# Narrowing all of the first float64 matrix before the experts, and a third of batch 1 with more row buffers, fewer stores and a later start

## The chip, the cores and the metric

One core of a Trainium2 chip runs the kernel. The metric is the device time of one execution in microseconds (us). Names of the engines: PE is TensorE, DVE is VectorE, ACT is ScalarE, POOL is GpSimd, SP is SyncE, which here only issues DMAs.

## The reference, cut to what matters

```python
X = np.fft.rfft(x, axis=1)                      # x: (4, 3072, 256) float32
Yr = Xr @ w_r - Xi @ w_i + b_r                  # and Yi, both 256 x 256
Yr = np.sign(Yr) * np.maximum(np.abs(Yr) - lam, 0.0)
y = np.fft.irfft(Y, n=3072, axis=1)             # back to tokens, 12288 x 256
expert_idx = np.argmax(y @ w_gate, axis=1)      # 8 experts, the first 384 tokens of each are kept
h = np.maximum(np.einsum('ecd,edf->ecf', disp, w1), 0.0)
out = gate_w * np.einsum('ecf,efd->ecd', h, w2) # 256 -> 1024 -> 256, other rows zero
h = x @ w_in                                    # the second network: w_in, w_out are float64
return (h * (1.0 / (1.0 + np.exp(-h))) @ w_out).astype(np.float32)
```

The last three lines work on the rows that the experts kept. `moe2_w_in` (256 x 2048) and `moe2_w_out` (2048 x 256) come as float64 and are read as pairs of 32-bit words.

## The kernel before

The work runs in this order. **First spectra** (`near`): batch 0 of x is loaded and taken through the first stage of the transform, then `kphase(0)` forms 24 spectra in 12 steps (`forward`, `shrink`, `back`: products with tables on PE, splits on ACT and DVE), beside `s1(1)`, the first stage of batch 1. The inverse of batch 0 follows (`is2`), with gate logits for each token, and beside it the first steps of `kphase(1)`. `route` and `rank` then choose the tokens of the first three experts, while PE works off the rest of `kphase(1)`. **Experts** (`experts`): each expert is 8 steps of `first_ffn` (tile `hp`, then `y`), with float32 products made of three matmuls by `mm3` (L208 to L210) from a high and a low part of either factor. Experts 0, 1 and 2 come first, then `second_ffn` works on pairs of experts (products `h`, then `o`), between which experts 3 to 7 run. Beside experts 0 to 2 runs `third(1)`: the inverse transform of the first third of batch 1, in 4 passes of `rows` (two loads `br` of 384 KB of the spectra in DRAM, `b_d`; eight products; a copy to `ao`; stores to `attn`) and `gate`, and then its `route`.

**Narrowing.** `narrow` turns 512 float64 columns into float32: a load into a buffer `nt` (three of them; the tile `mt` takes turns in the same three), `na` on ACT (L874), and on DVE L875, L879, L880 and L881. `ffn_in` does this for the 8 parts of `moe2_w_in` and splits them into `wi` (ACT, then POOL); for each second part it also forms sums and differences `mt` on DVE (L911 to L914), which are stored to `mixed`. Parts 0 to 3 run beside the first spectra, 4 and 5 beside `is2`, and 6 and 7 in `experts` (generator `fi`, advanced at the steps in `FIRST`). `ffn_out` does the same for the 8 parts of `moe2_w_out` into `wo`, at the steps in `AHEAD` and in the first `second_ffn`.

**Weights of the experts.** `weights` loads quarters of w1 and w2 (256 KB each) into `st`, of which there are four buffers; ACT casts the high part into `w`, DVE or POOL makes the low part (L200). The load of an expert's weights waits on SP for `idi`, the expert's number.

**The order of the work.** A scheduler puts the instructions of each engine into one fixed order when the kernel is built; a pin `after(a, b)` moves `a` behind `b` in it. Each engine then works off its list in order and waits at the head of the list. SP's list holds nearly all DMAs, so a DMA that waits there holds up all behind it. In `experts` the counter `n` (one per step of `first_ffn`, nine steps an expert) says when a piece of the side work is recorded: `due` and the numbers that `beside` yields for the third, `AHEAD` for `ffn_out`.

`turn(rows, zeros, ...)` transposes the gathered tokens of an expert (tile `gtp`); for the first expert it also records six products of zeros into `pw` (L1079), which nothing reads. `pair` prepares two experts' outputs for `second_ffn` (tiles `m1` to `m4`, `b2`).

Of the kernel before, what the change touches and what calls it, by code (L numbers as in the profile page):

```python
# [9 lines left out]
F32 = mybir.dt.float32  # L10
FR = mybir.dt.float32r
# [5 lines left out]
B, S, D = 4, 3072, 256  # L17
N1, N2 = 48, 64
NK = 24
Q = 96  # L20
TW = 32
E, F, CAP = 8, 1024, 384
# [14 lines left out]
WARM = 11  # L37
FIRST = 1, 4
AHEAD = 7, 10, 13, 16, 20
PMS = "vav"  # L40
# [10 lines left out]
def _tables():  # L51
# [23 lines left out]
    c1 = np.einsum("akr,pz->apkrz", c1, eye2).reshape(Q, Q)  # L75
    third = np.einsum("kra,pz->krpza", c4[:, :, :QB // 2], np.eye(2)).reshape(Q, QB)

# [40 lines left out]
    ind = ind.transpose(1, 0, 2).reshape(2, 2 * P)  # L118
    u, q = np.arange(P) // QB, 2 * (np.arange(P) % 16) + np.arange(P) // 16 % 2
    at = TW * q + GT * u  # L120
# [35 lines left out]
class Kernel:  # L156
# [96 lines left out]
    def near(self):  # L253

        ads, self.bds, self.res = {}, {}, {}
        self.left = ExitStack()
        self.kp = self.left.enter_context(self.tc.tile_pool(name="kpa", bufs=2, reuse_waits="tile"))
        with self.stream("a", 3, "right"), self.sums("a", 2):
            self.warm()
            self.first()  # L260
            tables, spectra = self.load_tables(), self.kphase(0, ads)
            for g in (tables, spectra, tables, spectra, spectra):
                next(g)
            mix([tables, spectra, self.s1(1, ads), self.ffn_in(0, 4)], [4, 10, 24, 10], lead=[0, 0, 0, 0])
            rest = self.kphase(1, ads, True)
            next(rest)
            with self.tc.issue_after(self.fetched):
                self.route_consts()
            mix([self.is2(0, (0, 1, 2), self.res), self.ffn_in(4, 6, 5)], [10, 7])
            self.route(0, (0, 1, 2), self.res)  # L270
            self.rank()
            self.early = self.slots(self.cst, 0, EARLY, self.sel, "s")[0]
            for _ in rest:
                pass
# [290 lines left out]
    def third(self, b, res):  # L565
# [4 lines left out]
        bv = self.bds[b].rearrange("k (r u g) c -> (k r) u (g c)", r=4, u=4)  # L570
        od = self.attn[0][b * S:b * S + QB * TW].rearrange("(t p u g) d -> u p t (g d)", p=2, u=4, g=GT)
        res[b] = self.chosen(1)
        def rows(n):
            pt = ps.tile([P, CH], F32, tag="ps", name="ps2")
            for w in range(2):
                br = bp.tile([Q, 2, CH], F32, tag="xt", name="br", bufs=self.sb)
                nc.sync.dma_start(out=br, in_=bv[:, 2 * w:2 * w + 2, n * CH:(n + 1) * CH])
                for z in range(2):
                    u = 2 * w + z
                    ins = nc.tensor.matmul(pt[u * QB:(u + 1) * QB], c4, br[:, z], start=True, stop=True).ins  # L580
                    if b == 1 and not u:
                        self.after(ins, self.lasty)
            ao = bp.tile([P, 2, 2, P], F32, tag="ao", name="ao2")
            aof = ao.rearrange("p g h d -> p (g h d)")
            nc.scalar.copy(aof, pt)
            for u in range(4):
                for p in range(2):
                    at = u * QB + p * (QB // 2)
                    nc.sync.dma_start(out=od[u, p, :, n * CH:(n + 1) * CH], in_=aof[at:at + QB // 2])
            return ao  # L590
# [29 lines left out]
    def is2(self, b, qbs, res):  # L620
# [29 lines left out]
        def turn(ao):  # L650
            aT = bp.tile([P, 2, NB, P], F32, tag="aT", name="aT")
            for h in range(2):
                tp = ps.tile([P, 4, P], F32, tag="ps", name="tp")
                for x in range(4):
                    nc.tensor.transpose(tp[:, x], ao[:, x % 2, x // 2, h * P:(h + 1) * P], self.ident)
                for ch in range(2):
                    v.tensor_copy(aT[:, h].rearrange("c b (o x t) -> c o b x t", o=2, x=4)[:, ch],
                                  tp.rearrange("c x (o b t) -> c o b x t", o=2, t=T)[:, ch, qbs[0]:qbs[0] + NB])
            return aT
# [233 lines left out]
    def ffn_in(self, q0, q1, late=LATE):  # L893
# [5 lines left out]
        for q in range(q0, q1):  # L899
            h, z = q % 2, (q // 2) * W  # L900
            a = self.ffn_part([(self.i["moe2_w_in"][h * P:(h + 1) * P, z:z + W], slice(0, W))], None if self.again else self.evicted or self.shrunk, None if self.again else self.gated.get(q))
            a = a.rearrange("p (i f m) -> p i f m", f=2, m=P)
# [23 lines left out]
    def experts(self, again=False):  # L926
# [17 lines left out]
        def beside():  # L944

            with self.stream("b", 2, "left"):
                yield 4
                for n, _ in enumerate(self.third(1, self.res)):
                    yield 5 + 2 * n
                tiny = self.mc.tile([P, 1], F32, name="tiny")  # L950
# [5 lines left out]

        fw, fi = self.ffn_out(), self.ffn_in(6, 8, 0)
        if again:
# [12 lines left out]
        xg = {e: self.gather(e) for e in order[:2]}  # L971
        xs[0] = self.turn(xg.pop(0), None if again else 6)
        ws = {e: self.weights(e, n) for e, n in zip(order[:2], (3, 4))}
# [3 lines left out]
        for at, ph in enumerate(order):  # L977
# [11 lines left out]
            for m, _ in enumerate(part):  # L989
# [4 lines left out]
                while due is not None and due <= n:  # L994
                    due = next(side, None)
                if n in FIRST:
                    next(fi, None)
                if n in AHEAD or (ph == E and m < 3):
# [8 lines left out]
                if m == 6 and after < E:  # L1007
                    xs[after] = self.turn(xg.pop(after), 0, behind)
            if ph < E and ph > 1 and ph % 2:
# [53 lines left out]

    def turn(self, rows, zeros=0, behind=None):
        xg, gw = rows
# [5 lines left out]
        for h in range(2):  # L1071
            tp = self.ph.tile([P, CAP], F32, tag="hp", name="gtp")
            for j in range(SC):
                last = self.nc.tensor.transpose(tp[:, j * P:(j + 1) * P], xg[:, j, h * P:(h + 1) * P], self.ident)
            self.split("av", xT[:, 0, h], xT[:, 1, h], tp)
        if zeros:
            pw = self.pm.tile([P, 2 * D], F32, tag="y", name="pw")
            for n in range(zeros):
                self.after(self.nc.tensor.matmul(pw[:, :D], self.zt[:, 0, :P], self.zt[:, 0], start=True, stop=True).ins, last.ins)  # L1079
        return xT  # L1080
# [28 lines left out]
    def pair(self, behind=None):  # L1109
# [8 lines left out]

        def cut(nm, src):
            t = mg.tile([P, 2, CAP], FR, name=nm, bufs=1)  # L1120
            self.split("av", t[:, 0], t[:, 1], src)
            return t[:, 0], t[:, 1]
# [5 lines left out]
        v.tensor_tensor(t2, b[:, 1], t1, ALU.subtract)  # L1128
        m2 = cut("m2", t2)
        v.tensor_tensor(b[:, 0], b[:, 1], b[:, 0], ALU.subtract)  # L1130
        m3 = cut("m3", b[:, 0])
        m1 = cut("m1", t1)
        v.tensor_tensor(a[:, 1], a[:, 1], t2, ALU.subtract)
        m4 = cut("m4", a[:, 1])
        b2 = cut("b2", b[:, 1])
        if behind:
# [215 lines left out]
```

## Time and profile before

| | |
|---|---|
| median of three runs | 623.26 us (622.26 to 624.34) |
| the profiled execution | 623.3 us, span 621.5 us |
| busy, share of the span | PE 598.7 us (96%), DVE 420.3 (68%), ACT 338.8 (55%), POOL 197.1 (32%) |
| mean granted clock of TensorE | 0.993 |
| DMA | 86.09 MB, mean 139 GB/s |

The median of the runs and the profiled execution agree within 0.1 us. The span is what the trace covers; the 1.8 us around it are in the time of the execution. An engine's idle time costs something only where PE, the busiest engine, ends up waiting for it.

### The profile page before, as it was taken

The page shows a single profiled execution, that of the slowest core. Times are in us where ns is not written, and L with a number is a line of the kernel's source. Part 1 is how long each engine was busy: PE and PEld are TensorE (multiplying, and loading weights), DVE is VectorE, ACT ScalarE, POOL GpSimd, SP SyncE. Part 2 cuts the span into 40 slices and gives each one's busy share as a digit, 9 for nine tenths or more (in the row PEclk, how much of TensorE's full clock was granted, in tenths as well). Part 3 has the DMA queues.
Part 4 walks back from the last instruction along what each step waited for, and adds up shares of the span by engine and source line. Part 5 has one row for each costly group of instructions (what it writes and reads, how often), then busy time and mean ns, then how long its engine had stood idle before and what let it go on. Part 6 is the DMA issues. An engine that isn't in the chain of part 4 may idle for free.

```text
span 621.5 us, 11504 instructions
## 1 busy us (share of the span) xinstructions
PE 598.7 (96%) x4128; PEld 557.0 (90%) x4128; DVE 420.3 (68%) x838; ACT 338.8 (55%) x722; POOL 197.1 (32%) x195
## 2 busy tenths in 40 slices
PE   9999999999999987989999999999999999999994
PEld 9887899668986766969999999999999999999993
DVE  2454875359967677999877687576577577485562
ACT  2535654346524545556766657556567555475561
POOL 1000110002064331456744504446403443163433
PEclk9999999999999998999999999999999999999998
DMA  8738865986266877910553533403433130010001
GB/s 207 198 98 247 293 201 153 243 245 212 69 200 196 226 191 260 310 51 26 152 183 123 155 119 112 161 26 119 145 127 110 51 126 26 13 65 26 16 2 55
DMA packets 66012, 86.09 MB, mean 139 GB/s; under 512 B 6069, under 2 KB 55865, under 8 KB 65945
## 3 DMA queue, kind: packets, MB, share of 16 engines
q1 hardware_dynamic: 53976, 69.53, 37.4%
q10 hardware_dynamic: 9664, 9.44, 5.1%
q0 software_dynamic: 2304, 6.29, 3.2%
q8 instruction: 34, 0.56, 0.4%
q14 instruction: 34, 0.27, 0.2%
HBM read 54.31 MB, written 30.93 MB: 137 GB/s over the span
## 4 chain that ended last, share of the span: by engine, by line
PE 80%; DVE 8%; issue 5%; DMA 4%; SPq 1%; ACT 1%; POOL 0%; POOLq 0%; DVEq 0%; ACTq 0%
PE o L209 7%; PE o L210 7%; PE o L208 7%; PE h L208 6%; PE h L210 6%; PE h L209 6%; PE hp L210 3%; PE hp L209 3%; PE hp L208 3%; PE y L210 3%; PE yp L208 3%; PE y L208 3%; PE y L209 3%; PE yp L210 3%; PE yp L209 3%
## 5 line engine op out<-in xcount | busy, mean ns | idle before, releaser
L1250 DVE TENSOR_TENSOR u<-h,u 128x384 f32<-128x384 f32 x224 | 117.4, 551 | 55.5 <-PE h L210 50.2
L1173 ACT ACTIVATE u<-u 128x384 f32<-128x384 f32 x128 | 64.1, 521 | 70.0 <-DVE u L1250 69.4
L209 PE MATMUL o<-wo,gl 128*128 128x256 f32 x366 | 98.1, 281 | 0.6 <-DVE gl L200 0.6
L210 PE MATMUL o<-wo,gh 128*128 128x256 f32 x366 | 98.0, 280 | 0.0
L208 PE MATMUL o<-wo,gh 128*128 128x256 f32 x366 | 86.2, 280 | 0.1
L200 POOL TENSOR_TENSOR ring<-mt,ring 128x384 fp32r<-128x384 f32 x32 | 38.2, 1195 | 131.7 <-ACT ring L192 131.6
L200 POOL TENSOR_TENSOR gl<-u,gh 128x384 fp32r<-128x384 f32 x62 | 64.9, 1065 | 30.7 <-ACT gh L192 28.2
L209 PEld LDWEIGHTS o<-wo,gl 128*128 128x128 f32 x366 | 68.8, 188 | 1.5 <-DVE gl L200 0.9
L210 PEld LDWEIGHTS o<-wo,gh 128*128 128x128 f32 x366 | 68.8, 188 | 0.0
L192 ACT CAST gh<-u 128x384 fp32r<-128x384 f32 x126 | 63.4, 510 | 5.1 <-PE o L210 3.5
L208 PEld LDWEIGHTS o<-wo,gh 128*128 128x128 f32 x366 | 64.4, 188 | 0.4 <-ACT gh L192 0.4
L208 PE MATMUL yp<-wri,xk 128*128 128x256 f32 x188 | 56.0, 298 | 0.0
L1096 ACT ACTIVATE hh<-hp 128x384 fp32r<-128x384 f32 x64 | 31.1, 490 | 43.4 <-PE hp L210 22.7
L200 POOL TENSOR_TENSOR wi<-na,wi 128x256 fp32r<-128x256 f32 (+1 forms) x8 | 8.7, 1085 | 143.7 <-ACT wi L192 143.7
L209 PE MATMUL yp<-wri,xk 128*128 128x256 f32 x188 | 53.7, 286 | 0.0
L210 PE MATMUL yp<-wri,xk 128*128 128x256 f32 x188 | 53.6, 285 | 0.0
L1097 DVE SCALAR_TENSOR_TENSOR hl<-hp,hh 128x384 fp32r<-128x384 f32 x64 | 35.0, 551 | 26.6 <-ACT hh L1096 23.1
L192 ACT CAST w<-st 128x512 fp32r<-128x512 f32 x64 | 38.8, 620 | 23.8 <-DMA st<-in_moe_w 16.0
L200 DVE TENSOR_TENSOR w<-st,w 128x512 fp32r<-128x512 f32 x53 | 36.6, 701 | 17.4 <-ACT w L192 17.2
L208 PE MATMUL y<-hh,w 128*128 128x384 f32 x128 | 44.1, 344 | 3.1 <-ACT hh L1096 3.1
L210 PE MATMUL hp<-xT,w 128*128 128x384 f32 x128 | 43.3, 339 | 0.6 <-DVE xT L200 0.6
L209 PE MATMUL hp<-xT,w 128*128 128x384 f32 x128 | 43.4, 339 | 0.4 <-DVE w L200 0.4
(254 smaller groups left out, 1541.5 us busy)
## 6 DMA issues: line engine op xcount, KB each, us to landing
st<-in_moe_w SPq DMA_DIRECT2D x64, 256.0 KB, 3.1
out<-zt SPq DMA_DIRECT2D x48, 256.0 KB, 3.1
b_d<-bo ACTq DMA_DIRECT2D x12, 512.0 KB, 3.9
mt<-mixed SPq DMA_DIRECT2D x32, 192.0 KB, 2.4
xt<-in_x SPq DMA_DIRECT2D x15, 384.0 KB, 7.2
nt<-in_moe_w_in SPq DMA_DIRECT2D x8, 512.0 KB, 4.9
nt<-in_moe_w_out SPq DMA_DIRECT2D x16, 256.0 KB, 5.0
a_d<-ao SPq DMA_DIRECT2D x8, 384.0 KB, 4.2
```

The lines of the kernel that those rows point to most:

```text
L192: self.lastact = self.nc.scalar.copy(dst, src)
L200: return e.tensor_tensor(dst, src, raw(hi), ALU.subtract).ins
L208: first = nc.tensor.matmul(out, lh, rh, start=start, stop=False)
L209: nc.tensor.matmul(out, ll, rh, start=False, stop=False)
L210: return first.ins, nc.tensor.matmul(out, lh, rl, start=False, stop=stop).ins
L1096: self.rectified = nc.scalar.activation(hh, hp, AF.Relu).ins
L1097: self.evicted = nc.vector.scalar_tensor_tensor(hl, hp, 0.0, raw(hh), ALU.max, ALU.subtract).ins
L1173: act.activation(sg, sg, AF.Silu)
L1250: v.tensor_tensor(to, h, u, ALU.add)
```

## The change

It does the following:

- `ffn_in` takes parts 0 to 5 beside the first spectra, starting at once, and parts 6 and 7 beside `is2`; none is left for the experts, and `FIRST` goes. Its pins are changed to suit.
- `ffn_out` is recorded at steps 2, 5, 8, 12 and 16 of the experts, where it was at 7, 10, 13, 16 and 20.
- The third of batch 1 begins at step 7, where it began at 4, and its stages come at 8, 10, 12, 14 and 16. Four of its eight row loads go into buffers of their own: three into a tile `bi` that shares its place with the tile `ms` of `pair`, one into `by` in the place of `yT`. So six loads can be in flight, where it was two.
- The tokens of the third stand in another order on the partitions (table `third`, and `tri` and `tok` to match), so each pass stores four blocks of 32 rows (64 KB) where it stored eight of 16 rows. To fit this order `turn` inside `is2` lets PE write each transposed block to every second column of the tile `tp`, and the copy `aT` reads runs of 32 numbers, where they were 16.
- The six products of zeros `pw` go.
- `m1` to `m4` and `b2` become one tile `ms`.

```diff
-FIRST = 1, 4
-AHEAD = 7, 10, 13, 16, 20
+AHEAD = 2, 5, 8, 12, 16
...
-    third = np.einsum("kra,pz->krpza", c4[:, :, :QB // 2], np.eye(2)).reshape(Q, QB)
+    third = np.einsum("kra,pz->krpaz", c4[:, :, :QB // 2], np.eye(2)).reshape(Q, QB)
...
-            mix([tables, spectra, self.s1(1, ads), self.ffn_in(0, 4)], [4, 10, 24, 10], lead=[0, 0, 0, 0])
+            mix([tables, spectra, self.s1(1, ads), self.ffn_in(0, 6, 0)], [4, 10, 24, 7], lead=[0, 0, 0, 0])
...
-            mix([self.is2(0, (0, 1, 2), self.res), self.ffn_in(4, 6, 5)], [10, 7])
+            mix([self.is2(0, (0, 1, 2), self.res), self.ffn_in(6, 8, 5)], [10, 7])
...
+        idle = self.mg.tile([P, 3, 2, CH], F32, tag="ms", name="bi", bufs=1)
+        room = {n + 2: idle[:Q, n] for n in range(3)}
+        room[5] = self.mh.tile([P, 2, CH], F32, tag="yT", name="by", bufs=1)[:Q]
...
-                br = bp.tile([Q, 2, CH], F32, tag="xt", name="br", bufs=self.sb)
+                br = room.get(2 * n + w)
+                if br is None:
+                    br = bp.tile([Q, 2, CH], F32, tag="xt", name="br", bufs=self.sb)
...
-                for p in range(2):
-                    at = u * QB + p * (QB // 2)
-                    nc.sync.dma_start(out=od[u, p, :, n * CH:(n + 1) * CH], in_=aof[at:at + QB // 2])
+                nc.sync.dma_start(out=od[u, :, n * CH:(n + 1) * CH], in_=aof[u * QB:(u + 1) * QB])
...
-                tp = ps.tile([P, 4, P], F32, tag="ps", name="tp")
+                tp = ps.tile([P, 2, P, 2], F32, tag="ps", name="tp")
...
-                    nc.tensor.transpose(tp[:, x], ao[:, x % 2, x // 2, h * P:(h + 1) * P], self.ident)
+                    nc.tensor.transpose(tp[:, x // 2, :, x % 2], ao[:, x % 2, x // 2, h * P:(h + 1) * P], self.ident)
...
-                yield 4
+                yield 7
                 for n, _ in enumerate(self.third(1, self.res)):
-                    yield 5 + 2 * n
+                    yield 8 + 2 * n
...
-        fw, fi = self.ffn_out(), self.ffn_in(6, 8, 0)
+        fw = self.ffn_out()
...
-        xs[0] = self.turn(xg.pop(0), None if again else 6)
+        xs[0] = self.turn(xg.pop(0))
...
-                if n in FIRST:
-                    next(fi, None)
...
-        if zeros:
-            pw = self.pm.tile([P, 2 * D], F32, tag="y", name="pw")
-            for n in range(zeros):
-                self.after(self.nc.tensor.matmul(pw[:, :D], self.zt[:, 0, :P], self.zt[:, 0], start=True, stop=True).ins, last.ins)
```

How the lists of the engines move. Lines below L35 are numbered one less in the new kernel than the same line before, and a few shift by some more. **SP, just ahead of the first weights of the experts** (`ar` and `mixed` end the spectra, `idi` is the expert's number, `st` its weights). Before:

```order
L868 DMA nt_2178<-in_moe2_w_in 128x1024
L868 DMA nt_2282<-in_moe2_w_in 128x1024
L423 DMA ar_1911<-a_d1_428 128x4x256
L916 DMA mixed_74<-mt_1362 128x2x384
L1029 TENSOR_LOAD idi_1484
```

Now:

```order
L919 DMA mixed_74<-mt_1392 128x2x384
L422 DMA ar_1941<-a_d1_428 128x4x256
L871 DMA nt_2218<-in_moe2_w_out 128x512 x2
L871 DMA nt_2311<-in_moe2_w_out 128x512 x2
L871 DMA nt_2465<-in_moe2_w_out 128x512 x2
L1030 TENSOR_LOAD idi_1514
```

The last two parts of `w_in` have gone ahead of this place, and the first three parts of `w_out` stand here, where they stood among the loads of experts 0 and 1.

**SP, the row loads of the third** (`br`, `bi`, `by`), beside the weights of expert 0's last quarter and expert 1 (`st`). Before:

```order
L577 DMA br_2264<-b_d1_1019 96x2x512
L577 DMA br_2268<-b_d1_1019 96x2x512
L1038 ISA
L1038 DMA st_2318<-in_moe_w1 128x2x256
L577 DMA br_2329<-b_d1_1019 96x2x512
L1038 ISA
L1038 DMA st_2323<-in_moe_w2 128x2x256
L589 DMA attn0_71<-ao2_2272 16x512 x8
```

Now:

```order
L582 DMA br_2383<-b_d1_1049 96x2x512
L582 DMA br_2387<-b_d1_1049 96x2x512
L1039 ISA
L1039 DMA st_2301<-in_moe_w1 128x2x256
L582 DMA bi_2380<-b_d1_1049 96x2x512 x3
L582 DMA by_2381<-b_d1_1049 96x2x512
L1039 ISA
L1039 DMA st_2306<-in_moe_w2 128x2x256
L1039 ISA
L1039 DMA st_2340<-in_moe_w1 128x2x256
```

Four row loads in a row, where there was one, stand ahead of the second half of that quarter (`st_2306`, before `st_2323`), and the first stores come later and are four.

**PE, at the products of zeros**, between the first two quarters of expert 0 and its first `y`. Before:

```order
L209 MATMUL hp<-xT,w_2170 128x384
L210 MATMUL hp<-xT,w_2170 128x384
L1079 MATMUL pw<-zt 128x256 x6
L208 MATMUL y_2155<-hh,w_2136 128x384
L209 MATMUL y_2155<-hh,w_2136 128x384
```

Now:

```order
L207 MATMUL hp<-xT,w_2193 128x384
L208 MATMUL hp<-xT,w_2193 128x384
L209 MATMUL hp<-xT,w_2193 128x384
L207 MATMUL y_2178<-hh,w_2159 128x384
L208 MATMUL y_2178<-hh,w_2159 128x384
```

The `y` products follow the `hp` products directly.

## Rows read from the trace of the kernel before

**Rows 1.** The page: span, busy time of each engine, granted clock in 40 slices.

```profile
span 621.5 us, 11504 instructions
...
PE 598.7 (96%) x4128; PEld 557.0 (90%) x4128; DVE 420.3 (68%) x838; ACT 338.8 (55%) x722; POOL 197.1 (32%) x195
...
PEclk9999999999999998999999999999999999999998
```

**Rows 2.** Stretches: length, PE, PEld, DVE, ACT, POOL busy, clock, DMA share, GB/s.

```profile
25.00:125.00 100.00, 100.00 (x701) 83.47 (x701) 57.64 (x101) 48.20 (x102) 5.83 (x6) 1.00 0.68 196
...
225.00:250.00 25.00, 20.57 (x116) 16.75 (x115) 18.67 (x41) 13.26 (x28) 9.20 (x7) 0.93 0.80 235
...
300.00:600.00 300.00, 300.00 (x2041) 298.90 (x2040) 206.23 (x385) 182.80 (x393) 117.31 (x109) 1.00 0.30 95
```

**Rows 3.** Waits of PE from 175 to 300 us: total, times, longest.

```profile
PE y L208 <- ACT hh L1096: 3.1, 2, 2.4
PE ps L580 <- DMA br<-b_d: 1.1, 3, 0.5
PE h L210 <- DVE m L200: 1.1, 1, 1.1
PE y L210 <- DVE hl L1097: 1.1, 1, 1.1
PE gtp L1074 <- DVE xg L1067: 0.9, 1, 0.9
PE tp L596 <- ACT ao L585: 0.9, 1, 0.9
```

**Rows 4.** Waits of ACT and of DVE from 205 to 245 us.

```profile
ACT w L192 <- DMA st<-in_moe_w: 9.7, 4, 4.8
...
DVE nsg L879 <- DMA nt<-in_moe_w_out: 5.8, 3, 2.1
```

**Rows 5.** Timeline of SP: the four groups of stores (start, length).

```profile
200.03 4.41 SPq L589 DMA_DIRECT2D attn<-ao  x8
...
211.72 7.41 SPq L589 DMA_DIRECT2D attn<-ao  x8
...
223.61 8.98 SPq L589 DMA_DIRECT2D attn<-ao  x8
...
238.33 5.51 SPq L589 DMA_DIRECT2D attn<-ao  x8
```

**Rows 6.** The tile `attn`: issue of its stores, ns minimum/median/maximum.

```profile
L589 SPq DMA_DIRECT2D attn<-ao x32: 302/303/1238, 200.0 to 243.5; - x32
```

**Rows 7.** Timeline of PE at the products of zeros and behind.

```profile
190.09 2.75 PE L1079 MATMUL pw<-zt 128*128 128x256 f32 x12
192.50 0.52 PE L208 MATMUL y<-hh,w 128*128 128x384 f32 x1
```

**Rows 8.** Stretches, columns as above: expert 0's start, the clock's fall, the first pair.

```profile
180.00:190.00 10.00, 8.02 (x41) 6.43 (x40) 7.95 (x15) 4.41 (x9) 6.88 (x6) 1.00 0.66 204
...
235.00:240.00 5.00, 2.15 (x20) 1.45 (x18) 1.43 (x5) 1.83 (x5) 0.00 (x0) 1.00 0.93 294
240.00:244.00 4.00, 3.51 (x11) 3.52 (x12) 3.91 (x8) 2.89 (x7) 1.69 (x1) 0.57 0.81 285
...
260.00:280.00 20.00, 17.12 (x102) 14.98 (x101) 19.76 (x45) 10.29 (x24) 9.25 (x8) 1.00 0.25 79
```

**Rows 9.** DVE, 186 to 207 us by line: busy us, mean ns.

```profile
L880 DVE SCALAR_TENSOR_TENSOR na<-na,nsg 128x512 int32<-128x512 int32 x2 | 3.5, 1766 | 0.0
...
L913 DVE TENSOR_TENSOR mt<-mt,na 128x256 f32<-128x256 f32 x1 | 1.5, 1514 | 0.0
```

**Rows 10.** DMA, 192 to 255 us: the queue that SP issues into.

```profile
q1 hardware_dynamic: 11444, 14.55, 79.0%
```

**Rows 11.** The tile `tp` in `is2`: ns minimum/median/maximum.

```profile
L655 PE MATMUL tp<-ident,ao x64: 272/273/332, 117.1 to 144.9; 128*128 128x128 f32 x64
```

More of the change, by code (lines that the diff above doesn't have):

```diff
@@ L118, in _tables @@
     ind = ind.transpose(1, 0, 2).reshape(2, 2 * P)
-    u, q = np.arange(P) // QB, 2 * (np.arange(P) % 16) + np.arange(P) // 16 % 2
+    u, q = np.arange(P) // QB, np.arange(P) % QB
     at = TW * q + GT * u
@@ L570, in third @@
         bv = self.bds[b].rearrange("k (r u g) c -> (k r) u (g c)", r=4, u=4)
-        od = self.attn[0][b * S:b * S + QB * TW].rearrange("(t p u g) d -> u p t (g d)", p=2, u=4, g=GT)
+        od = self.attn[0][b * S:b * S + QB * TW].rearrange("(q u g) d -> u q (g d)", u=4, g=GT)
         res[b] = self.chosen(1)
+        idle = self.mg.tile([P, 3, 2, CH], F32, tag="ms", name="bi", bufs=1)
+        room = {n + 2: idle[:Q, n] for n in range(3)}
+        room[5] = self.mh.tile([P, 2, CH], F32, tag="yT", name="by", bufs=1)[:Q]
         def rows(n):
@@ L652, in turn @@
             for h in range(2):
-                tp = ps.tile([P, 4, P], F32, tag="ps", name="tp")
+                tp = ps.tile([P, 2, P, 2], F32, tag="ps", name="tp")
                 for x in range(4):
-                    nc.tensor.transpose(tp[:, x], ao[:, x % 2, x // 2, h * P:(h + 1) * P], self.ident)
+                    nc.tensor.transpose(tp[:, x // 2, :, x % 2], ao[:, x % 2, x // 2, h * P:(h + 1) * P], self.ident)
                 for ch in range(2):
-                    v.tensor_copy(aT[:, h].rearrange("c b (o x t) -> c o b x t", o=2, x=4)[:, ch],
-                                  tp.rearrange("c x (o b t) -> c o b x t", o=2, t=T)[:, ch, qbs[0]:qbs[0] + NB])
+                    v.tensor_copy(aT[:, h].rearrange("c b (o x w) -> c o b x w", o=2, x=2)[:, ch],
+                                  tp.rearrange("c x (o b t) p -> c o b x (t p)", o=2, t=T)[:, ch, qbs[0]:qbs[0] + NB])
             return aT
@@ L900, in ffn_in @@
             h, z = q % 2, (q // 2) * W
-            a = self.ffn_part([(self.i["moe2_w_in"][h * P:(h + 1) * P, z:z + W], slice(0, W))], None if self.again else self.evicted or self.shrunk, None if self.again else self.gated.get(q))
+            a = self.ffn_part([(self.i["moe2_w_in"][h * P:(h + 1) * P, z:z + W], slice(0, W))], None if self.again else self.shrunk, None if self.again else self.gated.get(q - 3))
             a = a.rearrange("p (i f m) -> p i f m", f=2, m=P)
@@ L1007, in experts @@
                 if m == 6 and after < E:
-                    xs[after] = self.turn(xg.pop(after), 0, behind)
+                    xs[after] = self.turn(xg.pop(after), behind)
             if ph < E and ph > 1 and ph % 2:
@@ L1062, in gather, with turn @@
         return xg, gw
-    def turn(self, rows, zeros=0, behind=None):
+    def turn(self, rows, behind=None):
         xg, gw = rows
@@ L1073, in turn @@
             for j in range(SC):
-                last = self.nc.tensor.transpose(tp[:, j * P:(j + 1) * P], xg[:, j, h * P:(h + 1) * P], self.ident)
+                self.nc.tensor.transpose(tp[:, j * P:(j + 1) * P], xg[:, j, h * P:(h + 1) * P], self.ident)
             self.split("av", xT[:, 0, h], xT[:, 1, h], tp)
-        if zeros:
-            pw = self.pm.tile([P, 2 * D], F32, tag="y", name="pw")
-            for n in range(zeros):
-                self.after(self.nc.tensor.matmul(pw[:, :D], self.zt[:, 0, :P], self.zt[:, 0], start=True, stop=True).ins, last.ins)
         return xT
@@ L1117, in pair, with cut @@
             self.split("av", out[k][0], out[k][1], a[:, k])
-        def cut(nm, src):
-            t = mg.tile([P, 2, CAP], FR, name=nm, bufs=1)
+        ms = mg.tile([P, 5, 2, CAP], FR, tag="ms", name="ms", bufs=1)
+        def cut(n, src):
+            t = ms[:, n]
             self.split("av", t[:, 0], t[:, 1], src)
@@ L1128, in pair @@
         v.tensor_tensor(t2, b[:, 1], t1, ALU.subtract)
-        m2 = cut("m2", t2)
+        m2 = cut(0, t2)
         v.tensor_tensor(b[:, 0], b[:, 1], b[:, 0], ALU.subtract)
-        m3 = cut("m3", b[:, 0])
-        m1 = cut("m1", t1)
+        m3 = cut(1, b[:, 0])
+        m1 = cut(2, t1)
         v.tensor_tensor(a[:, 1], a[:, 1], t2, ALU.subtract)
-        m4 = cut("m4", a[:, 1])
-        b2 = cut("b2", b[:, 1])
+        m4 = cut(3, a[:, 1])
+        b2 = cut(4, b[:, 1])
         if behind:
```

## The prediction, as it was made before the run

> **What bounds the kernel now.** I read the page first. PE is busy for 598.7 of 621.5 us, and no other engine for more than 68% [rows 1], so a change can only win where PE waits, computes for nothing, or runs at the lower clock. The stretches tell where. From 25 to 125 us (first spectra) PE is never idle, and neither is it from 300 to 600 us [rows 2]; work taken away from other engines there wins nothing. The idle time that this change can reach lies between, in the experts 0 to 2 and at the first pair: from 225 to 250 us alone PE is busy for 20.57 of 25 us [rows 2]. The list of PE's waits says for whom: `y` for `hh` 3.1 us in two waits, `y` for `hl` 1.1, the third's transposes `tp` for the copy `ao` 0.9, its row products for the loads `br` 1.1 [rows 3]. [...]
>
> The waits of ACT and DVE say why these come late. Between 205 and 245 us ACT stands for 9.7 us before casts of expert weights that have not landed, and DVE for 5.8 us before the narrowing of `w_out` parts that have not landed [rows 4]. Both lists are in order, so `hh` and `hl` stand behind these. And the loads are late because SP's list carries them between the third's stores: four groups of eight take 4.41, 7.41, 8.98 and 5.51 us from first to last [rows 5], though the issue of one is 0.303 us in the median [rows 6].
>
> **The change part by part.** The sum is made against the profiled execution of 623.3 us (span 621.5), which is the median of the runs, 623.26, to 0.1 us.
>
> *Products of zeros, removed.* Twelve instructions from 190.09 to 192.50, where the next product, `y`, starts [rows 7]: 2.4 us on PE. By the timeline of ACT and DVE, what that `y` needs (weights and `hh`) was there before they ended, so I take 2.4 us as won. The bounds are 0 (the time becomes a wait) and 2.4. They may have held up the clock: before them PE is idle for 2.0 of 10 us at a granted clock of 1.00 [rows 8]. [...] I go by the row, since the products only fill time that real work now takes.
>
> *Parts 6 and 7 of `w_in`, moved out of the experts.* In expert 0 their narrowing costs DVE 3.5 us in L880 and 1.5 us in L913 alone [rows 9], with the rest of its lines between `hl`s. The first spectra get two more parts. There DVE is busy for 57.64 and ACT for 48.20 of 100 us [rows 2], and the first two loads now go out when the transfers of x end; the cover is the slack of DVE and ACT, and if it failed, `xk` would be late for PE. I charge 0.2 us.
>
> *Stores halved, `w_out` loads pulled ahead of the experts.* The four groups of stores take 4.41 + 7.41 + 8.98 + 5.51 = 26.3 us of SP's list [rows 5]. Half as many take between 16 x 0.303 = 4.8 us less, by the issue alone [rows 6], and 13.2 us less, half the groups; I take the upper end, since the groups show what SP really spends. Three parts of `w_out` (1.5 MB) leave the stretch from 192 to 255 us, where SP's queue moves 14.55 MB [rows 10], or 231 GB/s: 6.5 us of transfers. Each of the waits for weights and for `w_out` that hold `hh`, `hl` and `ao` is at most 4.8 us long [rows 4], so loads earlier by this much end them: 3.1 + 1.1 + 0.9 = 5.1 us of PE's waits [rows 3]. With the wait of 2.4 us goes the fall of the clock. In its stretch PE is busy for 3.51 us at 0.57 [rows 8], which costs 3.51 x 0.43 = 1.5 us.
>
> *More row buffers, third later.* The rows can't be loaded before batch 1's spectra are in DRAM, and that doesn't change; but PE now has three steps more of expert 0 before it needs them. The 1.1 us of waits for `br` [rows 3] go. Against this, four row loads now stand in one piece ahead of the second half of a weight quarter, three more than before: 3 x 384 KB at 231 GB/s are 5.1 us by which those weights and the ones behind may be late. The PE list puts some 24 expert products and a transposition ahead of the first that needs them. Between 0 and 5.1 us I take half, 2.5.
>
> *Ahead of the first expert.* The wait of `gtp` for the gathered tokens, 0.9 us [rows 3], stays: the change's list asks for the first tokens a little earlier and has spectra products behind. I charge 0.5 us, within a bound of 1.9 either way, which is nearly all that PE is idle there [rows 8].
>
> *The first pair.* From 260 to 280 us PE is idle for 20 - 17.12 = 2.9 us while DVE is busy for 19.76 of 20 [rows 8]; the largest wait there is `h` for a split of `pair`, 1.1 us [rows 3]. DVE comes to it with less left over from narrowing, but PE comes earlier too. I take half, 1.4 us, between 0 and 2.9. That `m1` to `m4` share one tile costs nothing: the next pair is prepared after the last one's products.
>
> *Transposes to every second column.* 64 instructions of 273 ns [rows 11], as many as before, with as many columns. No row shows PE writing with a step. The bounds are 0 and a start-to-start time doubled from some 0.147 us, which is 9.4 us; I take 0, because each still writes one number per column and partition.
>
> Sum: 2.4 + 5.1 + 1.5 + 1.1 + 1.4 - 0.2 - 2.5 - 0.5 = 8.3 us, so 623.3 - 8.3 = **615.0 us**. Its own range is 609.5 to 619.
>
> **The rivals.** *The bandwidth, not the list, holds the weights (0.15).* If SP's saved time only lets loads queue at the DMA engines, half of the 5.1 us and the clock's fall remain: 615.0 + 2.5 + 1.5 = 619. For it: from 235 to 240 us the DMA share is 0.93 at 294 GB/s [rows 8]. Against it: three `w_out` parts have left that stretch. [...]
>
> *DVE is the bound and takes it back (0.09).* If the first pair can't start earlier because `route` and `pair` fill DVE whatever PE does, what the experts win comes back as a wait there; only the products of zeros and part of a wait are won, and the charges take these: 622 to 623. For it: 19.76 of 20 us [rows 8]. Against: DVE stood for 5.8 us before loads [rows 4], and what it did not do then, it did here.
>
> *The burst of rows starves expert 0 and 1 (0.08, the other side).* Place: SP's list behind the four row loads; price: the weights come L later, PE waits for them, and a wait like that of 2.4 us brings one fall of the clock, 1.5 us. The waits of before stay, so only 2.4 + 1.1 = 3.5 us are won: 623.3 - 3.5 + L + 1.5. It is slower than before from L = 2.0 us on, and by over 0.3% from 3.9. With 5.1 us of rows and as much again as the stores' share, some 6.6 us, it gives 628.
>
> *The stepped transposes cost what their upper bound says (0.03):* 615.0 + 9.4 = 624.4.
>
> **How the numbers follow.** The forecast has 0.65, the rivals 0.15, 0.09, 0.08 and 0.03. A measurement of this kernel can tell about 0.3% (1.9 us) from no change. Faster by more, below 621.4: the forecast and the first rival, 0.80. Within it: the second and the last, 0.12. Slower: 0.08. The range reaches from 609.5, nearly all of the waits won, to 621.5, which takes in the first rival and part of the second.
>
> **What would show it.** Right: PE's busy time falls by 2 to 5 us and its wait for `hh` below 1 us; the granted clock is 1.00 from 225 to 250 us; no wait of DVE for `w_out` above 1 us; groups of four stores below 4 us each; expert 0 begins within 2 us of where it began, and the first `o` comes about 8 us earlier. From there on the traces run in parallel. Wrong, if PE waits for `w` around 200 us, if the first spectra show idle time of PE, or if `tp` takes longer than 273 ns each.

## The result, and the profile after

The changed kernel takes **615.84 us** in the median of six runs (613.65 to 618.49), the kernel before 622.95 beside it (622.21 to 625.84): a ratio of **0.988**, with a 95% interval from 0.985 to 0.991. 615.0 was forecast, so the sum came out. Its terms did not all: two came out wrong, two were missing, and these nearly cancelled. One execution of the kernel before and one of c_both (below) ran over 1.5% above the fastest of their kernel and are left out of the figures below.

The profiled execution has a span of 614.2 us, 7.3 less than before. The page:

```profile
span 614.2 us, 11459 instructions
...
PE 593.2 (97%) x4116; PEld 553.2 (90%) x4116; DVE 420.4 (68%) x838; ACT 338.7 (55%) x722; POOL 196.8 (32%) x195
...
PEclk9999999999999999999999999999999999999998
```

PE's busy time fell by 5.5 us [rows 1], but its idle time only from 22.8 to 21.0. Stretches of the span (columns as in [rows 2]):

```profile
25.00:125.00 100.00, 100.00 (x702) 83.47 (x702) 63.27 (x112) 50.70 (x107) 8.35 (x9) 1.00 0.71 207
125.00:150.00 25.00, 22.78 (x211) 14.57 (x211) 17.74 (x48) 11.93 (x25) 2.73 (x3) 1.00 0.69 211
...
200.00:205.00 5.00, 3.96 (x26) 2.47 (x25) 3.91 (x9) 1.90 (x5) 0.61 (x1) 1.00 1.07 249
205.00:210.00 5.00, 4.21 (x23) 3.56 (x21) 1.58 (x3) 1.77 (x4) 0.69 (x1) 1.00 1.08 260
210.00:215.00 5.00, 3.31 (x15) 1.70 (x15) 3.36 (x6) 2.69 (x6) 1.93 (x2) 0.78 1.09 272
215.00:220.00 5.00, 5.00 (x39) 3.80 (x35) 4.09 (x6) 2.80 (x6) 2.36 (x2) 0.88 0.94 250
225.00:250.00 25.00, 24.76 (x161) 21.98 (x158) 21.72 (x53) 13.19 (x29) 9.78 (x9) 1.00 0.82 258
...
250.00:275.00 25.00, 22.83 (x140) 21.02 (x139) 24.72 (x59) 13.89 (x30) 10.08 (x10) 1.00 0.21 64
```

The first spectra still leave PE no idle time, although DVE is busier there (63.27 us for 57.64). The stretch from 225 to 250 us, the worst before, is nearly full and runs at a clock of 1.00. In exchange there are new holes: 2.22 us from 125 to 150 us, where it was 0.57 (the row of before stands below), and 3.5 us from 200 to 215 us, with the DMA engines at a share above 1.0. Behind them the granted clock falls, to 0.78 and 0.88 in two stretches. So the fall of [rows 8] has not gone; it comes 28 us earlier. The inverse of batch 0 before:

```profile
125.00:150.00 25.00, 24.43 (x238) 17.51 (x236) 17.55 (x51) 12.46 (x28) 2.47 (x3) 1.00 0.76 227
```

The waits of PE from 195 to 215 us and, below the gap, from 25 to 150 us (total, times, longest):

```profile
PE y L207 <- ACT w L191: 1.8, 1, 1.8
PE hp L207 <- ACT w L191: 0.7, 1, 0.7
PE hp L207 <- DVE hl L1094: 0.5, 1, 0.5
PE y L209 <- DVE hl L1094: 0.3, 1, 0.3
...
PE lg L671 <- DVE aT L660: 1.2, 2, 0.7
PE tp L658 <- DVE L L557: 1.0, 1, 1.0
```

The waits for `hh`, `ao` and `br` [rows 3] are gone, and those for `hl` are 0.8 us. Those for `w`, 2.5 us, are new, and so are 2.2 us beside the inverse of batch 0, where parts 6 and 7 of `w_in` now make DVE late with `L` and `aT`. Behind the waits for `w` stand casts whose weights have not landed: ACT waits for `st` for 10.0 us between 205 and 245 us, where it was 9.7 [rows 4], and for 13.0 from 200 us on.

SP's list, the four groups of stores of the third:

```profile
208.11 3.58 SPq L592 DMA_DIRECT2D attn<-ao  x4
...
220.90 2.35 SPq L592 DMA_DIRECT2D attn<-ao  x4
...
225.28 2.06 SPq L592 DMA_DIRECT2D attn<-ao  x4
...
234.16 2.17 SPq L592 DMA_DIRECT2D attn<-ao  x4
```

They take 10.2 us, not 26.3 [rows 5]: half as many stores, and less than half the time. Why less than half shows in the waits of SP before, from 199 to 244 us, and in its list around the third group of stores:

```profile
SPq L589 <- DMA nt<-in_moe_w_out: 5.7, 10, 1.1
SPq L589 <- DMA br<-b_d: 3.7, 4, 1.1
SPq L589 <- DMA st<-in_moe_w: 2.9, 5, 1.0
```

```profile
219.37 1.06 SPq L1038 DMA_DIRECT2D st<-in_moe_w  x2
220.47 0.94 SPq L868 DMA_DIRECT2D nt<-in_moe_w_out  x2
221.52 0.37 SPq L577 DMA_DIRECT2D br<-b_d  x1
222.13 0.39 SPq L1038 DMA_DIRECT2D st<-in_moe_w  x1
222.57 0.47 SPq L868 DMA_DIRECT2D nt<-in_moe_w_out  x1
223.14 0.37 SPq L577 DMA_DIRECT2D br<-b_d  x1
223.61 8.98 SPq L589 DMA_DIRECT2D attn<-ao  x8
```

Of the 26.3 us, 12.3 are not issue but waits of stores for earlier loads to land. The last six stores of the third group wait, by the profile, for `nt`, `nt`, `br`, `st`, `nt` and `br`: in each case the DMA that stands eight places ahead in the list. In the trace the 276 DMAs of SP's list have eight semaphores between them, and each of these six stores waits for the DMA that had its semaphore before. The eight stores of a group have all eight, one each, so here a store of 32 KB took up one of eight places just as a load of 384 KB did.

A gain that the prediction doesn't have shows in PE's own products of the third. Timeline of PE before, the first four groups of row products, and of the change, its first and last:

```profile
196.76 1.05 PE L580 MATMUL ps<-br,c 96*32 96x512 f32 x4 [0.43 <-DMA br<-b_d]
198.32 1.05 PE L580 MATMUL ps<-br,c 96*32 96x512 f32 x4 [0.52 <-DMA br<-b_d]
...
203.35 1.05 PE L580 MATMUL ps<-br,c 96*32 96x512 f32 x4
...
208.66 1.05 PE L580 MATMUL ps<-br,c 96*32 96x512 f32 x4 [0.19 <-DMA br<-b_d]
```

```profile
202.01 1.11 PE L585 MATMUL ps<-br,c 96*32 96x512 f32 x8
...
229.31 1.06 PE L585 MATMUL ps<-br,c 96*32 96x512 f32 x8
```

Before, the four instructions of one load (two products, each of two) take 1.05 us, and the four of the pass's other load 1.05 us more at another time: eight such groups, 8.4 us. With the change both loads of a pass are there, the list puts all eight together, and they take 1.06 to 1.11 us: they write four different strips of 32 partitions of `ps2`, and PE overlaps them (in the first pass the products into all four strips start within 0.07 us). The four passes take 1.11, 1.94 (in the stretch of the lower clock), 1.24 and 1.06, together 5.4 us. That is 3.1 us won (8.42 - 5.35).

### The profile page after: what moved, and what is told of

It is laid out like the page before. It is cut to its first block, busy times and chain, and to the rows that moved or that the text cites. A ratio compares the mean times of both kernels' runs of the same rounds, so it can differ in the third digit from the quotient of the medians.

```text
span 614.2 us, 11459 instructions
## 1 busy us (share of the span) xinstructions
PE 593.2 (97%) x4116; PEld 553.2 (90%) x4116; DVE 420.4 (68%) x838; ACT 338.7 (55%) x722; POOL 196.8 (32%) x195
## 2 busy tenths in 40 slices
DMA packets 65755, 86.09 MB, mean 140 GB/s; under 512 B 5812, under 2 KB 55608, under 8 KB 65688
## 5 line engine op out<-in xcount | busy, mean ns | idle before, releaser
L199 DVE TENSOR_TENSOR w<-st,w 128x512 fp32r<-128x512 f32 x53 | 38.4, 734 | 18.5 <-ACT w L191 14.0
L207 PE MATMUL y<-hh,w 128*128 128x384 f32 x128 | 43.5, 341 | 1.8 <-ACT w L191 1.8
L207 PE MATMUL hp<-xT,w 128*128 128x384 f32 x128 | 43.4, 340 | 1.4 <-ACT w L191 0.7
L208 PE MATMUL y<-hh,w 128*128 128x384 f32 x128 | 43.3, 338 | 0.0
```

The lines of the kernel that those rows point to most:

```text
L199: return e.tensor_tensor(dst, src, raw(hi), ALU.subtract).ins
L207: first = nc.tensor.matmul(out, lh, rh, start=start, stop=False)
L208: nc.tensor.matmul(out, ll, rh, start=False, stop=False)
```

## The experiments

All were timed against the kernel before in five rounds. The interval of a ratio is about 0.0025 either way, so two kernels differ for certain only from some 0.004, 2.5 us, on. Each run also lists its mean granted clock, which scatters from 0.98 to 0.997 between runs of one kernel (a_layout). Time x (1 - clock) is my estimate, from these two figures of a run, of what the lower clock can have cost, at most, and time x clock is the rest. Both are means over the runs of a kernel, and the standard error of the last column is about 0.5 us or less where none is given. The kernel before alone has 619.0, 618.4 and 617.7 us there in the rounds of the runs a_zeros to a_ahead, a_noroom to b_layout, and c, so that between these groups a difference of 1 us says nothing.

| kernel | ratio to before (95%) | mean clock | time x (1 - clock) | time x clock |
|---|---|---|---|---|
| before (40 runs) | 1 | 0.991 | 5.3 | 618.4 |
| the change | 0.988 (0.985 to 0.991) | 0.993 | 4.4 | 611.4 |
| a_zeros | 0.994 (0.992 to 0.996) | 0.991 | 5.9 | 614.3 |
| a_layout | 0.993 (0.991 to 0.996) | 0.992 | 5.3 | 614.4 (1.2) |
| a_first | 0.987 (0.985 to 0.990) | 0.993 | 4.6 | 611.4 (0.7) |
| a_ahead | 0.992 (0.989 to 0.994) | 0.990 | 6.0 | 612.6 |
| a_noroom | 0.993 (0.990 to 0.995) | 0.992 | 4.7 | 614.3 |
| a_start4 | 0.989 (0.987 to 0.992) | 0.994 | 3.7 | 613.4 |
| b_nozeros | 0.997 (0.995 to 0.999) | 0.990 | 6.2 | 616.0 |
| b_layout | 0.992 (0.990 to 0.995) | 0.995 | 3.4 | 615.2 |
| c_laynoz | 0.992 (0.990 to 0.995) | 0.992 | 5.1 | 613.4 |
| c_all8 | 0.990 (0.987 to 0.994) | 0.990 | 6.2 | 610.9 (0.9) |
| c_rows | 0.987 (0.984 to 0.990) | 0.991 | 5.4 | 610.2 |
| c_both | 0.987 (0.984 to 0.991) | 0.993 | 4.4 | 610.4 (1.5) |

**The products of zeros** (a_zeros: back into the changed kernel; b_nozeros: taken out of the kernel before).

```diff
-        xs[0] = self.turn(xg.pop(0))
+        xs[0] = self.turn(xg.pop(0), None if again else 6)
```

> The changed kernel with the six products of zeros put back into `turn`, nothing else. Theory (the term of the sum, 2.4 us of PE): the twelve instructions push back all behind them, so the time is 615.8 + 2.4 = 618.2 us, 0.992 of before. Rival (they only fill a wait for the first weights, so the span from the first `hp` to the first `y` stays as long as it is): 615.8 us, 0.988. A fall of the clock that they prevent would show as a time below 615.8.

> The kernel before without the six products of zeros, nothing else. Theory (PE time of their own): 2.4 us less than 623, 0.996 of before. Putting them back into the changed kernel cost 0.6%; if that was more than their own time, because what is behind them is then late in other ways, it is 0.994 here too. Rival (they fill a wait): 1.000.

Putting them back costs 0.6% of the time before, some 3.9 us, and taking them out of the kernel before wins 0.3%, 1.8 us, with an interval from 0.5 to 3.1. With the clock taken out, that is 2.9 and 2.4 us. So they cost their own time, and the rival that they fill a wait falls. In a_zeros PE then waits 5.2 us for `w` in one piece. Whether they hold up the clock stays open: without them the cost of the lower clock is 0.9 us higher in b_nozeros (6.2 for 5.3), but with them it is 1.5 us higher in a_zeros (5.9 for 4.4).

**Half the stores** (a_layout: the old order of tokens in the changed kernel; b_layout: the new one alone in the kernel before).

```diff
-                for p in range(2):
-                    at = u * QB + p * (QB // 2)
-                    nc.sync.dma_start(out=od[u, p, :, n * CH:(n + 1) * CH], in_=aof[at:at + QB // 2])
+                nc.sync.dma_start(out=od[u, :, n * CH:(n + 1) * CH], in_=aof[u * QB:(u + 1) * QB])
```

> The changed kernel with the old order of tokens: eight stores of 16 rows for each pass of the third, and transposes in `is2` that write whole columns. Theory (SP's list holds the weights): SP gets back up to 13 us of stores and the weights of experts 0 and 1 come later, so PE waits 3 to 5 us more: 619 to 621 us, 0.994 to 0.997 of before. Rival (the DMA engines hold them; their share is 1.0 and more from 195 to 215 us in the trace of the change): within 1 us of 615.8, 0.987 to 0.990. If writing every second column of PSUM costs PE anything, the transposes of `is2` are shorter here than 273 ns.

> The kernel before with the new order of tokens alone: half the stores of the third, transposes of `is2` to every second column. Theory (SP's list holds the weights): 3 us less, 0.995 of before, as undoing it in the changed kernel cost 0.5%, and the wait of 2.4 us for `hh` at 240 us gets shorter. Rival (the loads of `w_out` and the narrowing of `w_in` in the experts hold `hh` here, whatever SP spends on stores): within 1 us, 0.9985 to 1.0015.

0.5% lost in the one (0.993, a little below the theory's 0.994 to 0.997), 0.8% won in the other: this part alone gives 4.7 us (interval 3.0 to 6.5), the largest share of the change. With the clock taken out it is about 3 us either way (614.4 for 611.4, 615.2 for 618.4). Before and in b_layout the DMA engines move the same 86.09 MB, in 66012 and 65755 packets; what differs is the list of SP. Its groups of stores in b_layout, and two stretches there:

```profile
199.53 1.70 SPq L587 DMA_DIRECT2D attn<-ao  x4
...
211.69 2.89 SPq L587 DMA_DIRECT2D attn<-ao  x4
...
222.24 3.21 SPq L587 DMA_DIRECT2D attn<-ao  x4
...
232.76 2.05 SPq L587 DMA_DIRECT2D attn<-ao  x4
```

```profile
200.00:225.00 25.00, 24.71 (x148) 19.00 (x147) 19.96 (x34) 14.77 (x31) 8.38 (x6) 1.00 0.95 280
225.00:250.00 25.00, 23.08 (x141) 20.37 (x140) 24.37 (x51) 14.72 (x31) 11.80 (x11) 1.00 0.94 292
```

26.3 us of SP's list became 9.9. The issue of one store takes 0.377 us in the median in b_layout, 6.0 us for the 16; so by this estimate the stores' waits fell from 12.3 to some 3.8 us, the rest from 14.0 to some 6.0. No wait of PE for `hh` is left in its list. The DMA engines move 292 GB/s instead of 235 in the second stretch, PE is idle there for 1.9 us instead of 4.4, and the clock stays at 1.00. So the DMA engines had room, and the list with its eight places kept it from them. What else the new order touches takes what it took: the transposes 273 ns and the copies `aT` 348 ns in the median with either order.

**The parts of `w_in`** (a_first, with the old pins and `FIRST` too).

```diff
-            mix([tables, spectra, self.s1(1, ads), self.ffn_in(0, 6, 0)], [4, 10, 24, 7], lead=[0, 0, 0, 0])
+            mix([tables, spectra, self.s1(1, ads), self.ffn_in(0, 4)], [4, 10, 24, 10], lead=[0, 0, 0, 0])
...
-            mix([self.is2(0, (0, 1, 2), self.res), self.ffn_in(6, 8, 5)], [10, 7])
+            mix([self.is2(0, (0, 1, 2), self.res), self.ffn_in(4, 6, 5)], [10, 7])
...
+                if n in FIRST:
+                    next(fi, None)
```

> The changed kernel with parts 6 and 7 of `w_in` narrowed in the experts again (at steps 1 and 4), 4 and 5 beside the inverse and 0 to 3 beside the first spectra, with the old pins. Theory (DVE's 9 us of narrowing stood before `hl` and the first pair): 2 to 3 us more, 618 to 619 us, 0.992 to 0.994 of before. Rival (DVE had room in the experts, and beside the inverse of batch 0 it hasn't: PE is idle for 2.2 us from 125 to 150 us with the change, 0.6 before): 1 to 1.6 us less, 614.2 to 614.8, 0.986.

No difference (0.987 and 0.988). Something of both expectations is seen. Without the move the inverse of batch 0 is undisturbed (PE idle for 0.7 us from 125 to 150 us, not 2.2), but PE waits 4.1 us for `hl` in the experts:

```profile
125.00:150.00 25.00, 24.32 (x239) 16.99 (x236) 16.99 (x50) 12.54 (x27) 1.80 (x3) 1.00 0.77 224
```

```profile
PE y L210 <- DVE hl L1097: 4.1, 2, 2.5
```

That is 3.3 us more for `hl` against 1.5 less at the inverse and 1.3 less at the first pair (`o` for `gl` 0.2, where the change has 1.5). Other waits move too, so that the two cancel is argued from these rows and not shown term by term.

**`w_out` ahead of the experts** (a_ahead).

```diff
-AHEAD = 2, 5, 8, 12, 16
+AHEAD = 7, 10, 13, 16, 20
```

> The changed kernel with `ffn_out` at steps 7, 10, 13, 16 and 20 again. Theory (1.5 MB ahead of the first weights keep the stretch of the experts free): 2 to 3 us more, 618 to 619 us, 0.992 to 0.994 of before. Rival (loads that early only fill the time in which SP and the DMA engines do little, and the later steps have room): within 1 us of 615.8, 0.987 to 0.990.

0.4% more, 2.3 us, as the theory had it, but the two intervals overlap, so this is not beyond the noise. With the clock taken out it is 1.2 us. Its profiled execution has the lower clock for twice as long from 200 to 225 us (a mean of 0.86 for 0.93 with the change), and PE waits of 2.4 us for `xT` and 1.9 us for `w`.

**Row buffers and start of the third** (a_noroom, a_start4).

```diff
-                br = room.get(2 * n + w)
+                br = None
```

```diff
-                yield 7
+                yield 4
...
-                    yield 8 + 2 * n
+                    yield 5 + 2 * n
```

> The changed kernel, but all eight row loads of the third use the two buffers `br` again (the third still starts at step 7). Theory (the burst of four row loads makes the weights of expert 0's last quarter late, a charge of 2.5 us, and the row buffers win 1.1 us): 1.4 us less than 615.8, 0.986 of before or lower, and PE's wait of 1.8 us for `w` at 209 us goes. Rival (without the buffers the rows come late, as the start is late too): 1 to 3 us more, 0.990 to 0.993, with waits of `ps` for `br`.

> The changed kernel with the third's old steps (begin 4, stages at 5, 7, 9, 11, 13) and the new row buffers. Theory (PE waits for the first rows, which can't come before batch 1's spectra are stored): the 1.1 us of waits for `br` come back, 617 us, 0.990 of before. Rival (with six loads in flight the start does not matter): within 0.5 us, 0.987 to 0.989. If the burst of rows is the cost, it comes earlier here and the first weights are later: 618 us and more.

Without the buffers it is slower by 0.5%, 2.9 us, so my theory falls, though what it said of PE is there: the waits for `w` at 203 to 211 us are gone. But so are the gains. Two of four passes go back to two groups of four instructions, of 1.05 us each. No wait for `br` of 0.3 us or more is in its list; the rival was right about the sign, not about the way. At the first pair PE is idle for more. Timeline of PE and a stretch in a_noroom:

```profile
212.29 1.05 PE L585 MATMUL ps<-br,c 96*32 96x512 f32 x4
...
217.51 1.05 PE L585 MATMUL ps<-br,c 96*32 96x512 f32 x4
```

```profile
250.00:275.00 25.00, 20.98 (x123) 18.84 (x123) 23.68 (x61) 12.00 (x26) 9.31 (x8) 1.00 0.20 63
```

PE is busy for 20.98 of 25 us from 250 to 275 us there, for 22.83 with the change, and the first `o` comes at 267.7 instead of 265.2 us. The earlier start alone changes nothing that can be told in the time (0.989), but the theory's wait is in its trace, and behind it the row products fall apart into groups of four again:

```profile
203.38 1.05 PE L585 MATMUL ps<-br,c 96*32 96x512 f32 x4 [1.59 <-DMA br<-b_d]
```

**The two losses, mended?** c_all8 narrows all of `w_in` beside the first spectra; c_rows issues the four extra row loads behind the second half (`quarter` is that load) of expert 0's last quarter; c_both does both.

```diff
-            mix([tables, spectra, self.s1(1, ads), self.ffn_in(0, 6, 0)], [4, 10, 24, 7], lead=[0, 0, 0, 0])
+            mix([tables, spectra, self.s1(1, ads), self.ffn_in(0, 8, 0)], [4, 10, 24, 9], lead=[0, 0, 0, 0])
...
-            mix([self.is2(0, (0, 1, 2), self.res), self.ffn_in(6, 8, 5)], [10, 7])
+            mix([self.is2(0, (0, 1, 2), self.res)], [10])
```

```diff
-                nc.sync.dma_start(out=br, in_=bv[:, 2 * w:2 * w + 2, n * CH:(n + 1) * CH])
+                ld = nc.sync.dma_start(out=br, in_=bv[:, 2 * w:2 * w + 2, n * CH:(n + 1) * CH])
+                if 2 * n + w in room:
+                    self.after(ld.ins, self.quarter)
```

> The changed kernel with all eight parts of `w_in` beside the first spectra, none beside the inverse of batch 0. Theory (parts 6 and 7 beside the inverse make `aT` late: PE is idle for 2.2 us from 100 to 150 us with the change and 0.6 before; undoing this part alone brought no time since it put the narrowing into the experts): 1.6 us less than the changed kernel, 0.985 of before, with no idle time of PE from 25 to 125 us. Rival (the first spectra have no room for two parts more on DVE or for the transfers): idle time of PE before 125 us, 0.988 or higher.

> The changed kernel with the four row loads into `bi` and `by` issued behind the second half of expert 0's last quarter (and so also behind the next load of weights). Theory (that burst makes the weights late: PE waits 1.8 and 0.7 us for `w` at 203 to 211 us and loses 1.7 us to the lower clock behind it): 2 to 4 us less than the changed kernel, 0.982 to 0.985 of before. Rival (the DMA engines are full from 195 to 215 us whatever the order, so another load is late in its place): within 1 us, 0.986 to 0.990.

> Both of the last two edits in one kernel. If each wins by its own theory: 0.979 to 0.982 of before. If neither does: 0.987 to 0.990.

None beats the change by more than can be told, as the rivals had it. In c_all8 the inverse is free of idle time, as meant, but the first spectra are not: PE waits there for a load of the transform's first stage (`ar`), ahead of which more loads of `w_in` now stand in SP's list. Stretches and the largest wait of c_all8:

```profile
25.00:125.00 100.00, 96.52 (x654) 82.47 (x654) 68.65 (x118) 50.27 (x108) 11.50 (x12) 0.98 0.71 206
...
125.00:150.00 25.00, 25.00 (x232) 15.85 (x230) 12.66 (x40) 10.67 (x21) 0.00 (x0) 1.00 0.67 190
```

```profile
PE xp L438 <- DMA ar<-a_d: 2.3, 1, 2.3
```

In c_rows the wait for `w` shrinks to 0.2 us, and others take its place, from 195 to 260 us:

```profile
PE hp L207 <- DVE xT L199: 2.9, 2, 2.7
PE y L207 <- ACT hh L1097: 1.1, 1, 1.1
```

From 195 to 215 us PE is busy for 16.6 of 20 us there, for 16.5 with the change, at 261 and 263 GB/s. So at this place the order of these loads is not what holds PE; it only chooses who waits. That the DMA engines do is argued from their share of about 1 and not shown: no run here took bytes out of that stretch without changing something else, and a share of about 1 is no one rate (from 250 to 260 us the kernel before has 1.06 at 373 GB/s). In the change SP waits there as well, 8.0 us in sum, for row loads and weights ahead in its list to land.

**Two parts without the other four** (c_laynoz: the kernel before with half the stores and without zeros, the edits of b_layout and b_nozeros together).

> The kernel before with two of the six parts of the change: the new order of tokens (half the stores) and no products of zeros. Alone they gave 0.992 and 0.997. Theory (they carry nearly all of the change, and the other parts together move idle time rather than remove it): 0.988 to 0.990. Rival (the row buffers and the earlier `w_out`, which cost 0.4 to 0.5% each when undone, are needed): 0.992 or higher. Removing the zeros may bring back a fall of the clock, of which the kernel with the new order alone showed none before 600 us; then 0.991.

0.992, no better than b_layout alone, and 0.4% behind the whole change. With the clock taken out the zeros are worth 1.8 us here too (613.4 for 615.2; 1.1 if each is taken against the kernel before in its own rounds), and the lower clock takes it back (5.1 us for 3.4): its profiled execution has two falls (a mean clock of 0.93 from 175 to 200 us and again from 200 to 225), where b_layout's has none before the end (1.00 in every stretch to 600 us). Its row products are eight groups of four again, one of them behind a wait of 1.5 us for `br`. So the rival is right and some of the four other parts are needed: together they give the last 2.7 us, just beyond the noise.

## Why the prediction was right, point by point

- **Products of zeros, 2.4 us:** right. By the runs 1.1 to 2.9 us with the clock taken out.
- **Stores halved, `w_out` ahead:** halving the stores was the right lever and alone is worth 4.7 us. SP's list got back 16 us, more than the 13.2 at the upper end, because the reading behind the two bounds was wrong: I took the length of the groups for what SP spends on its stores, and 12.3 of the 26.3 us were waits for a place. The `w_out` loads moved are 1.57 MB, 6.8 us at 231 GB/s and not 6.5; a_ahead can't tell what they won from nothing.
- **`hh`, `hl`, `ao`, 5.1 us:** 0.8 us of it is left, so 4.3 were won as waits. The rival on bandwidth may be half right: b_layout shows that SP's list held the loads before, but in the changed kernel, with six row loads issued in one stretch, the DMA engines have a share of 1.06 from 195 to 215 us. In the trace of before a store's issue takes 0.303 us in the median [rows 6] and 3.9 us pass until it has landed; of the 8.98 us for eight [rows 5], 5.2 were waits for earlier loads to land.
- **`br` 1.1 us, and weights late 2.5 us:** the waits for `br` went, and PE waits 1.8 + 0.7 = 2.5 us for `w`, as charged. That a half of 5.1 hit it is luck, and the reason was wrong or incomplete: loads in another order (c_rows) only move the wait.
- **The clock, 1.5 us:** this step failed. I let the fall go with the longest wait, which was an estimate from [rows 3] and [rows 8]; it came at another place, behind a shorter wait of 1.8 us with smaller ones around it (a mean clock of 0.78 from 210 to 215 us and of 0.88 from 215 to 220). No run shows which wait brings a fall. Over all runs the lower clock cost 5.3 us before and 4.4 now, 0.9 less, with an error near that size.
- **Parts 6 and 7 of `w_in`:** the charge of 0.2 us for the first spectra was right (no idle time). Missing was the inverse of batch 0: I costed the two parts beside it at nothing, as two other parts had stood there before, though these are pinned elsewhere, and it lost 1.6 us of PE.
- **Row buffers:** missing was the overlap of the eight row products, 3.1 us. The trace of before shows the groups of four; I priced only the wait.
- **First pair, 1.4 us:** the waits there went from 2.9 us to 2.1 (`o` for `gl` 1.5, `h` for `u` 0.6), so 0.8.
- **Transposes 0, `gtp` 0.5:** 273 ns as before; in the trace the four of a group start 0.109 us apart in the median before and now, not 0.147, so the rival's 9.4 us should have been 7.0. `gtp` waits 0.9 us as before, and spectra beside it wait 0.5 for `bo`.
- **The signs:** most came (`hh`, `w_out`, the stores, the clock from 225 to 250 us, the first `o`). PE's busy time fell by 5.5 us, just outside 2 to 5. Two went the other way: PE waits for `w` around 200 us, which was named as a sign of being wrong, and the first product of expert 0 comes 4.1 us later, where 2 were allowed, since more products of the spectra stand ahead of it in PE's list. Timeline of PE before, and now:

```profile
183.01 0.52 PE L208 MATMUL hp<-xT,w 128*128 128x384 f32 x1
```

```profile
187.07 0.53 PE L207 MATMUL hp<-xT,w 128*128 128x384 f32 x1
...
193.01 0.33 PE L207 MATMUL y<-hh,w 128*128 128x384 f32 x1
```

So although the zeros are gone the first `y` starts 0.5 us later than before [rows 7]. The whole gain lies between it and the first `o`: 72.2 us instead of 80.8. Behind that 0.8 us are lost again.

Taken together from the two profiled executions: zeros 2.4, waits in the experts 4.3, `br` 1.1, row products 3.1, first pair 0.8, against `w` 2.5, the inverse 1.6 and 0.5 beside `gtp`: 7.1 us, where the span fell by 7.3. Smaller waits that I left out move some half a microsecond either way, so the agreement is no better than that. The first `o` came at 265.2 instead of 273.3 us, the 8 us forecast. That the total of 8.3 was near is partly luck: the missing 3.1 us made up for the clock's 1.5 and the inverse's 1.6.

The likeliest of the other rivals, DVE taking everything back, fell: the first pair's span from its first `h` to the first `o` got shorter, from 12.0 to 8.5 us. No kernel tried was slower than the one before.

## What to carry to other kernels

A list of DMAs on one engine is a resource of its own: here the 276 DMAs of SP's list before have eight semaphores between them, a store of 32 KB took up one of eight places, and 12.3 of the 26.3 us of the stores were waits for a place. Merging stores into fewer instructions, by choosing the order of rows on the partitions, was worth 4.7 us alone, more than any move of loads, with every byte the same. Before calling the time of an issuing engine issue, look at what it waits for. When work moves, look at both ends: what it freed at the old place (waits for `hl`, 4.1 us to 0.8) and whom it disturbed at the new one (2.2 us beside the inverse, among others) left no difference in the time. And where inputs arrive in pairs, see whether PE can take the products side by side, as it did here with eight instructions in 1.06 us, where four took 1.05.

## What the runs showed of the hardware that was not expected

- The row products that write different strips of 32 partitions overlapped on PE where they stood next to each other: eight instructions of 96 x 512 float32 took 1.06, 1.11 and 1.24 us in the three passes at a clock of 1.00, four took 1.05.
- A DVE instruction took up to 1783 ns beside POOL, where its median is 693. The 3.5 us that I had for L880 in the experts [rows 9] were two instructions of some 1.77 us. Of the 16 in the kernel before, the five that start while a POOL instruction is under way take 908 to 1783 ns and the eleven others 676 to 693, also where POOL starts behind them. For example, one starts at 188.11, while POOL works from 187.78 to 189.34:

```profile
188.11 1.78 DVE L880 SCALAR_TENSOR_TENSOR na<-na,nsg 128x512 int32<-128x512 int32 x1
```

```profile
187.78 1.56 POOL L200 TENSOR_TENSOR w<-st,w 128x512 fp32r<-128x512 f32 x1 [1.25 <-ACT w L192]
```

  An estimate from these rows: if it waited until POOL was done and then took its 0.69 us, it would end at 190.03; it ended at 189.89. So a wait for POOL fits to 0.14 us; the cause is not shown.
- The clock differs between runs of one kernel: its mean went from 0.984 to 0.997 (c_rows), with times of 618.1 and 612.9 us.
